# First batch's loads in groups of eight tiles, dummy matmuls among the column sums, and a third weight product on the first exponentials

## The chip, the cores and the metric

The kernel runs on one core of one Trainium2 chip. The time is the device time of one execution in microseconds (us). Before the change it is 813.8 us (median; single executions of the measurement 813.60 to 813.84). A time here is about 1.8 us longer than the span of the same execution's trace.

## The reference

Four batches. In each, a 256 x 256 channel attention: q and k are normalized over the 6016 tokens, their product goes through a softmax, and v is multiplied by it. The result goes through a gated feed-forward block.

```python
qn = q / (norm(q, axis=1) + 1e-6);  kn = k / (norm(k, axis=1) + 1e-6)   # B, N, C = 4, 6016, 256
a = softmax(kn.transpose(0, 2, 1) @ qn / tau)
x = (v @ a).reshape(B * N, C)
out = (silu(x @ w_gate) * (x @ w_val)) @ w_out                          # d_ff = 1536
```

## The kernel before

The softmax matrix is folded into the gate and value weights (`wp_matmul`), so that the tokens see only the feed-forward matmuls. Batches 1 to 3 get their softmax in the background of the batch before. The first batch can't: its k and q (12.3 MB in fp32) are loaded and cast to fp8 first, and TensorE waits for them. q and k have 47 tiles of 128 tokens; a load takes 4 tiles. All are issued from GpSimd, in this order:

```python
groups = [(s, min(4, NS - s)) for s in range(0, NS, 4)]            # NS = 47
qgroups = groups[:-1] + [(s, min(2, NS - s)) for s in range(gs, NS, 2)]
order = [k groups ...] + [q groups ...]                             # 12 + 13 loads
for ...: load_qk(0, g, which, gl)
load_first_v()
load_w(0, HW); load_w(HW, WP)         # gate and value columns 0-255, 256-511
load_v(*allc[1])                      # second chunk of v
for wc in range(1, NWC):              # first of these: "wg1", gate columns 512-1023
    load_w(wc * WP, (wc + 1) * WP)
```

As the groups land, ScalarE and VectorE square them (`first_square`), TensorE forms the logits (`gemm1_pair`, q only) and the sums of squares: with a matrix of ones for k and the first 36 tiles of q (`first_row_sums`), as columns for q's last 11 tiles (`first_col_sums`). Then comes the softmax and the first weight products:

```python
row_eps(rs); transpose_first_v(); keep_warm(3)     # keep_warm: dummy matmuls of 512 columns
... two exponentials on ScalarE ...
row_sum(0)
wp_matmul(b, 0, 0, units[0], lo); wp_matmul(b, 1, 0, units[1], lo)
row_sum(1)
... the other products, evacuations, then the feed-forward loop
```

Of the kernel before, what the change touches and what calls it, by code (L numbers as in the profile page):

```python
# [17 lines left out]
def kernel(  # L18
# [17 lines left out]
    CH = C // P  # L36
    FH = DFF // P
    NS = N // P
# [14 lines left out]
    groups = [(s, min(4, NS - s)) for s in range(0, NS, 4)]  # L53
# [45 lines left out]
    def load_qk(b, g, which, gl=groups):  # L99
        if b not in qk_tiles:  # L100
            q_sb = qkpool.tile([P, NS, C], FP8, tag="q_sb")
            k_sb = qkpool.tile([P, NS, C], FP8, tag="k_sb")
            qk_tiles[b] = (q_sb, k_sb)
        gs, gm = gl[g]
        src, dst = (q, k)[which], qk_tiles[b][which]
        nc.gpsimd.dma_start(  # L106
            out=dst[:, gs:gs + gm, :],
            in_=src[b].rearrange("(p s) c -> p s c", s=NS)[:, gs:gs + gm, :])
# [17 lines left out]
    def transpose_first_v():  # L126
        vt_ps = psum_o.tile([P, CH, CS * P], BF16, tag="o")
        for h in range(CH):
            for j in range(CS):
                nc.tensor.transpose(vt_ps[:, h, j * P:(j + 1) * P],  # L130
                                    v0_sb[:, j, h * P:(h + 1) * P], ident)
        state["vt_ps"] = vt_ps
        vT_new = vpool.tile([P, CH, CS * P], BF16, tag="vT")
        vt_ready[(0, 0)] = vT_new

    def evacuate_first_v(h):
        nc.vector.tensor_copy(vt_ready[(0, 0)][:, h, :], state["vt_ps"][:, h, :])
# [43 lines left out]
    def first_row_copy(b):  # L181
        row = work.tile([1, C], FP32, tag="row")
        nc.vector.tensor_copy(row, state[b, "ss", 0][0:1, :])
        state[b, "row"] = row
# [21 lines left out]
    def first_root(dst, src):  # L206
        nc.scalar.activation(dst, src, ACT.Ln)
        nc.scalar.activation(dst, dst, ACT.Exp, scale=0.5)
# [7 lines left out]
    def first_inv_k(b, n):  # L216
        part = state[b, "ink"][:, n * (C // 4):(n + 1) * (C // 4)]
        nc.vector.reciprocal(part, part)

    def first_softmax(b):  # L220
        kq, ink = state[b, "kq"], state[b, "ink"]
        inq = work.tile([P, CH], FP32, tag="inq")
        first_root(inq, state[b, "cols"])
        s_f = work.tile([P, CH, C], FP32, tag="s_f")
        nc.vector.tensor_mul(s_f[:, 0, :], kq[:, 0, :], ink)
        nc.vector.tensor_scalar_add(inq, in0=inq, scalar1=1e-6)
        nc.vector.reciprocal(inq, inq)
        if inv_tau != 1.0:
            nc.vector.tensor_scalar_mul(inq, in0=inq, scalar1=inv_tau)
        nc.vector.tensor_mul(s_f[:, 1, :], kq[:, 1, :], ink)  # L230
        rs = psum_m.tile([P, CH], FP32, tag="misc")
        row_eps(rs)
        transpose_first_v()
        keep_warm(3)
        for h in range(CH):
            evacuate_first_v(h)
        exT = attn.tile([P, CH, C], BF16, tag="exT")
        state[b, "exT"] = exT
        for jh in range(CH):
            nc.scalar.activation(exT[:, jh, :], s_f[:, jh, :], ACT.Exp,  # L240
                                 scale=inq[:, jh:jh + 1])


        def row_sum(jh):
            for ih in range(CH):
                nc.tensor.matmul(rs[:, ih:ih + 1], exT[:, jh, ih * P:(ih + 1) * P],
                                 ones_bf[:, 0:1], start=False,
                                 stop=(jh == CH - 1), skip_group_check=True)

        units = []  # L250
        for u in range(2 * CH):
            unit_ps = psum_gv.tile([P, HW], FP32, tag="gv"[u % 2])
            units.append(unit_ps)
        row_sum(0)
        wp_matmul(b, 0, 0, units[0], lo)
        wp_matmul(b, 1, 0, units[1], lo)
        row_sum(1)
        finish_rs(b, rs)
        wp_matmul(b, 0, 1, units[0], lo)
        wp_matmul(b, 1, 1, units[1], lo)  # L260
        for u in (2, 3):
            for jh in range(CH):
                wp_matmul(b, u, jh, units[u], lo)
        for u in range(4):
            wp_evacuate(b, u, units[u], lo, u % 2 == 1)
        for u in range(2):
            wp_unit(b, u, psum_o, "o", hi)
        nc.scalar.preload_act_table(ACT.Silu)
# [85 lines left out]
    def row_eps(rs):  # L354

        nc.tensor.matmul(rs, ones_f[0:1, :], eps[0:1, :], start=True, stop=False,
                         skip_group_check=True)
# [10 lines left out]
    def finish_rs(b, rs, eps=0.0):  # L368
        smr = work.tile([P, CH], FP32, tag="smr")
        if eps:  # L370
            nc.vector.tensor_scalar_add(smr, in0=rs, scalar1=eps)
            nc.vector.reciprocal(smr, smr)
        else:
            nc.vector.reciprocal(smr, rs)
        Wg = attn.tile([P, CH, DFF], BF16, tag="Wg")
        Wv = attn.tile([P, CH, DFF], BF16, tag="Wv")
        state[b, "smr"], state[b, "W"] = smr, (Wg, Wv)

    def keep_warm(n):
        ps = psum_o.tile([P, 2, C], FP32, tag="o")  # L380
        for _ in range(n):
            nc.tensor.matmul(ps, ones_bf, warm_bf, start=True, stop=True)
# [4 lines left out]
    full, lo, hi = slice(0, WP), slice(0, HW), slice(HW, WP)  # L387

    def wp_matmul(b, u, jh, ps, part):
        wc, w, ih = wp_units[u]  # L390
        cols = slice(wc * WP + part.start, wc * WP + part.stop)
        nc.tensor.matmul(ps, state[b, "exT"][:, jh, ih * P:(ih + 1) * P],  # L392
                         (w_gate_sb, w_val_sb)[w][:, jh, cols],
                         start=(jh == 0), stop=(jh == CH - 1))

    def wp_evacuate(b, u, ps, part, on_dve):
        wc, w, ih = wp_units[u]
        scale = state[b, "smr"][:, ih:ih + 1]
        cols = slice(wc * WP + part.start, wc * WP + part.stop)
        dst = state[b, "W"][w][:, ih, cols]  # L400
        if on_dve:
            nc.vector.tensor_scalar_mul(dst, in0=ps, scalar1=scale)
        else:
            nc.scalar.activation(dst, ps, ACT.Copy, scale=scale)

    def wp_unit(b, u, pool=psum_m, tag="misc", part=full, on_dve=None):

        ps = pool.tile([P, part.stop - part.start], FP32, tag=tag)
        for jh in range(CH):
            wp_matmul(b, u, jh, ps, part)  # L410
        wp_evacuate(b, u, ps, part, u % 2 == 1 if on_dve is None else on_dve)
# [117 lines left out]
    VT_AHEAD = 2  # L529


    NG = len(groups)
    gs, gm = groups[-1]
    qgroups = groups[:-1] + [(s, min(2, NS - s)) for s in range(gs, NS, 2)]
    NQ = len(qgroups)
    order = [(g, 1, groups) for g in range(NG)] + [(g, 0, qgroups) for g in range(NQ)]
    for n, (g, which, gl) in enumerate(order):
        load_qk(0, g, which, gl)
        if n == 8:
            make_identity(nc, identf)  # L540
            nc.gpsimd.memset(half, 0.5)
            nc.gpsimd.memset(minus, -1.0)
# [6 lines left out]
    nc.gpsimd.dma_start(out=w_out_sb, in_=moe_w_out.rearrange("(h l) d -> l h d", l=P))  # L549
    G_COLS = NQ - 4  # L550
    T_COLS = qgroups[G_COLS][0] // 2
    for g, which, gl in order:
        gs, gm = gl[g]
        ts = list(range(gs // 2, (gs + gm + 1) // 2))
        if which == 0 and g == NQ - 1:
            continue
        if which == 0 and g == NQ - 2:

            gs, gm = gl[g + 1]
            ts += range(gs // 2, (gs + gm + 1) // 2)  # L560
        if which == 0 and g == G_COLS:
            first_row_copy(0)
        sqs = [first_square(0, t, which, on_dve=(t % 2 == 1)) for t in ts]
        if which == 0:
            for t in ts:
                gemm1_pair(0, t)
            if g == G_COLS:
                first_cols(0)
        for t, sq in zip(ts, sqs):
            if which == 0 and g >= G_COLS:  # L570
                first_col_sums(0, t, sq)
            else:
                first_row_sums(0, t, which, sq, (T_COLS if which == 0 else NP) - 1)
        if which == 0:
            if g == 0:
                first_norm_k(0)
                nc.vector.tensor_copy(ident, identf)
            elif g <= 4:
                first_inv_k(0, g - 1)
    first_softmax(0)  # L580
    prev = None
    for gi, (b, ci) in enumerate(allc):
# [56 lines left out]
```

## Time and profile before

| | before |
|---|---|
| time, median | 813.8 us |
| span of the trace | 811.9 us |
| TensorE busy | 98% |
| last landing of q | 34.07 us |
| wg1 landed, TensorE continuous from there | 40.55 us |
| TensorE's wait for wg1 | 0.38 us |

The lines that this rests on are in the prediction. One more view matters afterwards: the windows view over stretches of 3.41 us, which is the step in which the granted clock changes in these traces. The columns are the stretch, its length, busy us (and instructions) of TensorE, weight loads, VectorE, ScalarE, GpSimd, then the granted clock, DMA share and GB/s written.

```profile
25.06:28.47 3.41, 3.14 (x24) 2.12 (x22) 2.71 (x5) 1.89 (x3) 1.59 (x3) 1.00 1.11 104
28.47:31.89 3.42, 2.94 (x20) 1.85 (x19) 1.65 (x4) 1.26 (x2) 1.61 (x3) 1.00 1.12 108
31.89:35.30 3.41, 3.13 (x40) 2.62 (x40) 2.38 (x5) 2.23 (x5) 2.51 (x4) 1.00 1.26 167
35.30:38.71 3.41, 3.28 (x30) 2.29 (x32) 2.88 (x9) 2.39 (x7) 3.23 (x6) 1.00 1.27 205
```

TensorE is busy for 2.94 us or more of each 3.41 us while it waits for q, and the clock is whole (1.00).

### The profile page before, as it was taken

To read this page: it belongs to the slowest core of one execution; us is meant where nothing else is said; L and a number is where in the kernel's file an instruction comes from. 1 tells how busy PE (TensorE), PEld (TensorE's weight loads), DVE (VectorE), ACT (ScalarE), POOL (GpSimd) and SP (SyncE) were. 2 spreads that over 40 slices of the span, in tenths; PEclk is the share of its full clock that TensorE was granted. 3 is DMA by queue.
4 is the path that set the end of the run, shared out by engine and by line. 5 is a ranking of instruction groups with operands and counts; after the bars stand their busy time and mean duration, and the time that the engine had idled before them with its cause. 6 is when DMAs were issued, how large, how long until landed. Compare 5 with 4: busy or idle time off the path is not lost.

```text
span 811.9 us, 13668 instructions
## 1 busy us (share of the span) xinstructions
PE 794.1 (98%) x4952; PEld 488.9 (60%) x5042; DVE 524.3 (65%) x795; ACT 434.8 (54%) x757; POOL 267.2 (33%) x330
## 2 busy tenths in 40 slices
PE   5999999999999999999999999999999999999998
PEld 3656666665565666666565666666556565665666
DVE  4777777657556777656755677765765555555554
ACT  4666655545555556545555556654554544444543
POOL 5515887423000888722100488752300000000000
PEclk9999999999999999999999999999999999999999
DMA  9993875329312678334912377641942112112101
GB/s 87 142 157 69 115 105 86 80 34 150 77 40 46 96 100 106 74 65 95 127 40 59 53 96 112 89 78 37 171 102 66 46 50 55 52 40 65 50 27 59
DMA packets 93747, 64.99 MB, mean 80 GB/s; under 512 B 52896, under 2 KB 92448, under 8 KB 92928
## 3 DMA queue, kind: packets, MB, share of 16 engines
q0 software_dynamic: 19584, 27.41, 29.0%
q1 hardware_dynamic: 73952, 36.65, 18.2%
q8 instruction: 39, 0.64, 0.4%
q14 instruction: 28, 0.23, 0.1%
q10 hardware_dynamic: 144, 0.07, 0.0%
HBM read 79.04 MB, written 36.70 MB: 143 GB/s over the span
## 4 chain that ended last, share of the span: by engine, by line
PE 93%; DMA 4%; issue 1%; DVE 1%; POOL 0%; ACT 0%; POOLq 0%
PE o_new L457 30%; PE v_ps L423 30%; PE g_ps L423 28%; DMA q_sb<-in_q_dram 2%; PE ps L392 2%; PE kq_new L151 2%; DMA k_sb<-in_k_dram 1%; DMA w_gate_sb<-in_moe_w_gate_dram 1%; DVE sv L433 0%; POOL k_sb L106 0%; ACT silu L429 0%; PE last_ps L481 0%; POOL vb L114 0%; DVE sq L274 0%; PE kq_new L156 0%
## 5 line engine op out<-in xcount | busy, mean ns | idle before, releaser
L433 DVE TENSOR_TENSOR sv<-silu,v_ps 128x512 bf16<-128x512 bf16 (+1 forms) x576 | 388.3, 674 | 263.9 <-ACT silu L429 261.1
L429 ACT ACTIVATE silu<-g_ps 128x512 bf16<-128x512 f32 (+1 forms) x576 | 338.7, 588 | 323.4 <-PE g_ps L423 257.5
L457 PE MATMUL o_new<-w_out_sb,sv 128*128 128x256 bf16 x2244 | 337.2, 273 | 1.5
L423 PE MATMUL v_ps<-vT,Wv 128*128 128x512 bf16 (+1 forms) x1100 | 324.3, 374 | 2.9
L423 PE MATMUL g_ps<-vT,Wg 128*128 128x512 bf16 (+1 forms) x1074 | 319.1, 375 | 0.3
L457 PEld LDWEIGHTS <-sv 128*128 128x128 bf16 x2244 | 219.6, 98 | 140.6
L423 PEld LDWEIGHTS <-Wv 128*128 128x128 bf16 x1152 | 112.7, 98 | 130.7
L284 POOL TENSOR_TENSOR acc_new<-acc_new,sq 128x512 f32<-128x512 f32 x135 | 157.6, 1167 | 45.1 <-DVE sq L274 36.9
L423 PEld LDWEIGHTS <-Wg 128*128 128x128 bf16 x1152 | 109.7, 98 | 24.9
L274 DVE TENSOR_TENSOR sq<-q_sb 128x512 bf16<-128x512 fp8e5 x72 | 65.9, 915 | 0.0
L279 POOL TENSOR_TENSOR acc_new<-sq 128x512 f32<-128x512 bf16 x3 | 3.5, 1154 | 150.5 <-DVE sq L274 150.5
L275 ACT ACTIVATE sq<-k_sb 128x512 bf16<-128x512 fp8e5 x72 | 44.2, 614 | 0.0
L466 ACT COPY o_sb<-o_new 128x512 f32<-128x512 f32 x48 | 28.1, 586 | 14.9 <-PE o_new L457 14.5
L151 PE MATMUL kq_new<-k_sb,q_sb 128*128 128x512 fp8e5 x184 | 32.0, 295 | 0.5 <-DMA q_sb<-in_q_dram 0.5
L106 POOL DMA_DIRECT2D q_sb<-in_q_dram x49 | 27.4, 558 | 13.5 <-DMA k_sb<-in_k_dram 5.5
L468 DVE COPY o_sb<-o_new 128x512 f32<-128x512 f32 (+1 forms) x47 | 31.3, 666 | 0.0
L106 POOL DMA_DIRECT2D k_sb<-in_k_dram x48 | 26.0, 542 | 10.4 <-DMA w_out_sb<-in_moe_w_out_dram 5.6
L178 PE MATMUL ss_new<-sq,ones_bf 128*128 128x256 bf16 x83 | 17.8, 353 | 9.1 <-ACT sq L168 8.6
L114 POOL DMA_DIRECT2D vb<-in_v_dram x47 | 24.1, 515 | 5.3 <-DMA vb<-in_v_dram 4.1
L151 PEld LDWEIGHTS <-q_sb 128*128 128x256 fp8e5 x184 | 21.2, 138 | 2.6 <-DMA q_sb<-in_q_dram 2.0
L178 PEld LDWEIGHTS <-ones_bf 128*128 128x128 bf16 x83 | 9.9, 122 | 15.9 <-issue 11.6
L312 POOL TENSOR_TENSOR inv<-inv,half 128x4 f32<-128x4 f32 x3 | 3.1, 1036 | 36.7 <-DVE inv L311 36.7
(94 smaller groups left out, 195.9 us busy)
## 6 DMA issues: line engine op xcount, KB each, us to landing
out_dram<-o_sb SPq DMA_DIRECT2D x92, 256.0 KB, 2.5
vb<-in_v_dram POOLq DMA_DIRECT2D x43, 256.0 KB, 5.9
k_sb<-in_k_dram POOLq DMA_DIRECT2D x44, 128.0 KB, 5.9
q_sb<-in_q_dram POOLq DMA_DIRECT2D x44, 128.0 KB, 5.1
w_out_sb<-in_moe_w_out_dram POOLq DMA_DIRECT2D x1, 768.0 KB, 13.7
vb<-in_v_dram POOLq DMA_DIRECT2D x4, 192.0 KB, 3.5
vT<-vb SPq DMA_TRANSPOSE x47, 4.3
w_gate_sb<-in_moe_w_gate_dram POOLq DMA_DIRECT2D x2, 256.0 KB, 7.0
```

The source lines that it names most:

```text
L106: nc.gpsimd.dma_start(out=dst[:, gs:gs + gm, :], in_=src[b].rearrange("(p s) c -> p s c", s=NS)[:, gs:gs + gm, :])
L151: nc.tensor.matmul(kq[:, jh, :], q_sb[:, ps:ps + 2, js], k_sb[:, ps:ps + 2, :], start=(t == 0 and jh == 0), stop=last, perf_mode=DR, skip_ ...
L178: nc.tensor.matmul(state[b, "ss", which], ones_bf, sq[:, s, :], start=(t == 0 and s == 0), stop=(t == t_last and s == pm - 1))
L274: nc.vector.tensor_mul(sq[:, :pm, 0, :], q_sb[:, ps:ps + pm, :], q_sb[:, ps:ps + pm, :])
L275: nc.scalar.activation(sq[:, :pm, 1, :], k_sb[:, ps:ps + pm, :], ACT.Square)
L284: nc.gpsimd.tensor_tensor(out=acc, in0=acc, in1=sq[:, s, :, :], op=ALU.add)
L423: nc.tensor.matmul(dst[:, :mv], W[:, kk, fs], vT[:, kk, :mv], start=(kk == 0), stop=(kk == CH - 1))
L429: nc.scalar.activation(silu[:, :mv], g_ps[:, :mv], ACT.Silu)
L433: nc.vector.tensor_mul(sv[:, f, :mv], silu[:, :mv], v_ps[:, :mv])
L457: nc.tensor.matmul(self.o_ps[:, j % 2, :], self.sv[:, f, j * P:(j + 1) * P], w_out_sb[:, f, :], start=(f == 0), stop=(f == FH - 1))
L466: nc.scalar.copy(o_sb[:, :m, :], self.o_ps[:, :m, :])
L468: nc.vector.tensor_copy(o_sb[:, :m, :], self.o_ps[:, :m, :])
```

## The change

The intent: fewer loads on the queue that bounds the start, TensorE kept at full clock in the thinner column-sum stage, and one more product in the wait for the second exponential.

```diff
-    qgroups = groups[:-1] + [(s, min(2, NS - s)) for s in range(gs, NS, 2)]
+    kgroups = [(s, min(8, NS - s)) for s in range(0, NS, 8)]
+    ...  size = 8 if rest >= 16 else 4 if rest >= 4 else min(2, rest)   # q: 8 8 8 8 4 4 4 2 1
@@ first_softmax
+        keep_warm(1)
         row_eps(rs)
         transpose_first_v()
-        keep_warm(3)
+        keep_warm(2)
@@
         wp_matmul(b, 1, 0, units[1], lo)
+        wp_matmul(b, 2, 0, units[2], lo)
         row_sum(1)
         ... (the remaining products follow, as before)
@@ loop over the groups
+            if G_COLS <= g < NQ - 2:
+                keep_warm(1)
```

More of the change, by code (lines that the diff above doesn't have):

```diff
@@ L256, in first_softmax @@
         wp_matmul(b, 1, 0, units[1], lo)
+        wp_matmul(b, 2, 0, units[2], lo)
         row_sum(1)
         finish_rs(b, rs)
-        wp_matmul(b, 0, 1, units[0], lo)
-        wp_matmul(b, 1, 1, units[1], lo)
-        for u in (2, 3):
-            for jh in range(CH):
-                wp_matmul(b, u, jh, units[u], lo)
+        for u, jh in ((0, 1), (1, 1), (2, 1), (3, 0), (3, 1)):
+            wp_matmul(b, u, jh, units[u], lo)
         for u in range(4):
@@ L529 @@
     VT_AHEAD = 2
-    NG = len(groups)
-    gs, gm = groups[-1]
-    qgroups = groups[:-1] + [(s, min(2, NS - s)) for s in range(gs, NS, 2)]
-    NQ = len(qgroups)
-    order = [(g, 1, groups) for g in range(NG)] + [(g, 0, qgroups) for g in range(NQ)]
+    kgroups = [(s, min(8, NS - s)) for s in range(0, NS, 8)]
+    qgroups, at = [], 0
+    while at < NS:
+        rest = NS - at
+        size = 8 if rest >= 16 else 4 if rest >= 4 else min(2, rest)
+        qgroups.append((at, size))
+        at += size
+    NG, NQ = len(kgroups), len(qgroups)
+    order = [(g, 1, kgroups) for g in range(NG)] + [(g, 0, qgroups) for g in range(NQ)]
     for n, (g, which, gl) in enumerate(order):
         load_qk(0, g, which, gl)
-        if n == 8:
+        if n == 4:
             make_identity(nc, identf)
```

## The prediction

> **What bounds the kernel now.** I read the page first. Its head, busy time and chain say that TensorE is the bound of the whole program, but that four hundredths of the span belong to transfers:
>
> ```profile
> span 811.9 us, 13668 instructions
> PE 794.1 (98%) x4952; PEld 488.9 (60%) x5042; DVE 524.3 (65%) x795; ACT 434.8 (54%) x757; POOL 267.2 (33%) x330
> PE 93%; DMA 4%; issue 1%; DVE 1%; POOL 0%; ACT 0%; POOLq 0%
> ```
>
> 811.9 us of span stand for 813.82 us of time; the 1.9 us between them I take as constant. The change touches only the first batch, so next I read the chain in order of time over the first 75 us:
>
> ```profile
> 1.22 3.34 POOL k_sb L106 x6
> 4.56 8.36 DMA k_sb<-in_k_dram
> 12.92 0.28 issue
> 13.21 9.44 DMA q_sb<-in_q_dram
> 22.64 0.28 issue
> 22.93 10.19 DMA q_sb<-in_q_dram
> 33.12 0.28 issue
> 33.40 0.53 POOL vb L114
> 33.93 0.10 issue
> 34.03 6.52 DMA w_gate_sb<-in_moe_w_gate_dram
> 40.55 0.04 issue
> 40.60 1.04 PE ps L392 x4
> 41.63 0.43 PE g_ps L423 x2
> ```
>
> The reader is to see one border, at 40.55 us. Before it nothing but loads sets the pace: k, q, then the load of the gate weights' columns 512 to 1023, which is called wg1 here. After it TensorE runs without a gap, and nothing of the change reaches there. So the change is worth exactly what it moves wg1's landing, as long as TensorE has come to its wait before that. The timeline gives the slack (columns: start us, us, engine, line, operation, then what it waited for):
>
> ```profile
> 38.75 0.60 PE L392 MATMUL ps<-w_val_sb,exT 128*128 128x256 bf16 x4
> 39.62 0.59 PE L423 MATMUL v_ps<-vT_new,Wv 128*128 128x512 bf16 x2
> 40.60 1.04 PE L392 MATMUL ps<-w_gate_sb,exT 128*128 128x512 bf16 x4 [0.38 <-DMA w_gate_sb<-in_moe_w_gate_dram]
> ```
>
> TensorE stood idle for 0.38 us before wg1: that is all that work on TensorE could grow by without cost, and work taken away there gives nothing. Last, two stretches of the windows view (busy us of each engine, granted clock, DMA share, GB/s written) and the GpSimd issues in the timeline:
>
> ```profile
> 15.00:20.00 5.00, 4.31 (x18) 2.44 (x18) 2.55 (x5) 2.52 (x4) 2.16 (x5) 1.00 1.13 104
> 25.00:30.00 5.00, 4.64 (x35) 3.17 (x33) 3.46 (x6) 2.52 (x4) 2.50 (x4) 1.00 1.13 108
> ...
> 20.47 0.53 POOL L106 DMA_DIRECT2D q_sb<-in_q_dram  x1 [0.71 <-DMA q_sb<-in_q_dram]
> 21.68 0.53 POOL L106 DMA_DIRECT2D q_sb<-in_q_dram  x1 [0.68 <-DMA q_sb<-in_q_dram]
> ...
> 30.50 0.70 POOL L524 DMA_DIRECT2D w_gate_sb<-in_moe_w_gate_dram  x1 [0.53 <-DMA q_sb<-in_q_dram]
> ```
>
> The transfer engines are never empty (share over 1, packets overlap), and their 104 GB/s of fp8 written are 416 GB/s of fp32 read. Each GpSimd issue waits for the landing of the load eight issues before it: from 20.47 to 30.50 us eight landings of 4 tiles come at a pitch of (30.50 - 20.47) / 8 = 1.254 us. So loads in flight are plenty, and the bound of this stage is the rate of the queue.
>
> **What the Trainium skill says.** "DMA: Bandwidth & Descriptors", section Specifications, has a fabric ceiling of 435 GB/s over 16 engines. The trace agrees: a 4 KB read takes 173 ns, a 1 KB read 60 ns in the packet records, which is 37.7 ns per KB and engine, 16 x 1024 B / 37.7 ns = 435 GB/s, plus 22 ns. The same page, Rules for kernel authors, asks for at least 1 MiB per DMA; a 4-tile load reads 512 KB, an 8-tile load 1 MiB. But its fit of about 2.0 us fixed plus bytes over 436 GB/s is for one DMA alone (section Anatomy of one DMA); with eight in flight this trace shows only 1.254 us per 512 KB, so nearly all of that fixed part is hidden already, and the rule's gain with it. "TensorE: Matmul & The Clock Gate", Part 1, says that the array runs at half clock until it has been busy for a window of about 3.4 us, and falls back after an idle one. The trace agrees on the first: the four row-sum matmuls of a load span 1.01 us until 20 us and 0.60 us from 24 us on; the clock's record starts at 21.65 us. It never falls before the end.
>
> **The change, part by part.**
>
> Loads of eight. k goes from 12 loads to 6, q from 13 (eleven of 4 tiles, then 2 and 1) to 9 (8, 8, 8, 8, 4, 4, 4, 2, 1): ten loads fewer, the same bytes. What a load costs beside its bytes comes from the landing records, as the first engine sees them: pitch 1.254 us for 4 tiles, 0.96 for 3, 0.66 for 2, 0.34 for 1. The slope is (1.254 - 0.34) / 3 = 0.305 us per tile (eight packets of 1 KB of source per engine at 37.7 ns make 0.301), so the rest is 1.254 - 4 x 0.305 = 0.035 to 1.254 - 4 x 0.301 = 0.05 us per load. I choose 0.04, and check it on the value chunk's load, 512 KB in one 32 KB read per engine, which lands 1.24 after its predecessor: even very long packets gain only 0.015. Ten loads fewer: 10 x 0.04 = **0.4 us**, all of it on the path: last q landing from 34.07 to 33.7 us, wg1 from 40.55 to 40.15. The weight loads that follow are unchanged in count, order and size. Issues wait for the load eight before, as now, so the queue holds more bytes, not fewer; GpSimd's 0.53 us per issue stays hidden, and is paid ten times less.
>
> Granularity. The last fifteen q tiles keep their 4, 4, 4, 2, 1, so what follows the last landing is as before. In the stages ahead an 8-tile group comes each 2 x 1.254 - 0.04 = 2.47 us. ScalarE and VectorE have two squares each in it, 2 x 0.63 and 2 x 0.69 us. TensorE has 8 logits matmuls and 8 row sums, twice what a 4-tile group has, at full clock 2 x (0.5 + 0.43) = 1.9 us; at half clock about 4 us. The first q group lands 1 us later (21.2 instead of 20.2 us), finds TensorE cold, and a backlog of one or two us builds until the clock rises, somewhere from 24.6 to 28 us. At a gain of 0.6 us per group it is worked off by the column sums unless the window falls badly. The four buffers of squares now are one group, not two; squares start again as row sums free them.
>
> Dummy matmuls. One each after the column sums of two groups, 0.22 us at full clock, in gaps where TensorE waits for q (the chain shows loads there); the second may push the last logits matmuls by up to 0.2 us. One moves ahead of the transposes, where TensorE now waits 0.26 us for v: hidden, and it leaves two instead of three after them, 0.2 us off the way to the first row sum. Together about zero.
>
> Third product. The two exponentials take 0.91 us from 35.77 us, so TensorE waits for the second until 36.68 us; with one dummy fewer there is room of 0.4 us, which the two old products fill by 0.2. The third (0.11 us) fits, and is 0.11 us less afterwards. It stands ahead of the wait for wg1, so it adds to the 0.38 us of slack and not to the time.
>
> Sum: 813.82 - 0.4 - 0 - 0 = **813.4 us**.
>
> **The rivals.**
>
> (a) Long packets run much better, as the rule of 1 MiB suggests, and the stage gains 1 us or more. Against it: at 0.301 us per tile the 25 loads can't take less than 47 x 2 x 0.301 = 28.3 us, and from the first landing on they take 28.6 us at the slowest engine for the 90 tiles after the first load, 0.6 of which an instruction fetch of 16 KB took at 30 us from one engine. There is no microsecond to win but that one. If the fetch falls on an engine that is ahead (the engines' landings of one load lie 0.75 us apart), some 0.5 us more come: 812.9.
>
> (b) TensorE becomes the bound: cold for longer in q, or throttled again between bursts of 2.5 us, so that it reaches wg1's wait late. If it warms at 28 us, it is 0.9 us late at the last q group; less 0.38 of slack that costs 0.5: 813.9. A fall of the clock at the softmax would cost more, some 1 to 1.5 us: 814.5. For it: 68% busy in the k stage didn't raise the clock. Against it: the clock never fell in the column-sum stage of before, and the dummies were put there for it.
>
> (c) The loads gain, but a new wait for another load sets the start, and nothing moves: 813.8. The weight loads stand in the same queue behind q and move with it, so I hold this for unlikely.
>
> **Range and chances.** The middle is 813.4; rival (a) with the fetch bounds it at 812.8 below, (b) in its mild form at 814.0 above; the runs of before lie within 0.24 us. 2% would be 16 us, and the whole stage before 40.55 us holds no such amount to win and no mechanism to lose it. Faster 0.01, same 0.98, slower 0.01.
>
> **What would show it.** Right: the chain still changes from loads to TensorE at a wait for wg1, near 40.15 us; GpSimd issues in the k stage at a pitch of 2.46 to 2.48 us; TensorE waits there 0.2 to 0.6 us; the third product lies ahead of the second row sum, without delaying it by more than 0.1 us. Wrong: a pitch under 2.4 us (packets gain more than their fixed part), the chain running through logits matmuls or column sums in 22 to 35 us (rival b), a granted clock under 1 after 28 us, or wg1's landing unmoved though the pitch fell (rival c).

## The result

| | before | changed |
|---|---|---|
| executions, us | 813.60 813.72 813.77 813.81 813.82 813.84 | 813.38 813.44 813.67 813.73 815.01 815.38 |
| median, us | 813.79 | 813.70 |
| ratio | | 1.0004 (95% interval 0.9991 to 1.0017) |
| span of the trace, us | 811.9 | 811.6 |

A ratio is the mean time of one kernel's runs over that of the other's in the same rounds, so it isn't quite the ratio of the medians. Here the means are 814.10 and 813.76 us: the two executions at 815 pull the ratio over 1, though four of six are faster than the median of before, and two of these faster than all of it. Executions over 1.5% slower than the fastest of the same kernel are left out of the means.

The profile of the changed kernel (813.38 us). First the page's first line and the shares of the chain:

```profile
span 811.6 us, 13660 instructions
PE 93%; DMA 4%; issue 1%; DVE 0%; POOL 0%; ACT 0%; POOLq 0%
```

Then pieces of the chain in order of time (start us, us, what):

```profile
3.50 12.81 DMA k_sb<-in_k_dram
16.59 16.18 DMA q_sb<-in_q_dram
...
33.70 6.58 DMA w_gate_sb<-in_moe_w_gate_dram
40.29 0.05 issue
40.33 1.04 PE ps L391 x4
```

The form is that of before: loads up to wg1, then TensorE. The border went from 40.55 to 40.29 us, by 0.26, and the span from 811.9 to 811.6. Next, in the timeline, two issues of GpSimd, the third product with the row sum behind it, and TensorE's wait for wg1:

```profile
14.14 0.53 POOL L106 DMA_DIRECT2D q_sb<-in_q_dram  x1 [1.95 <-DMA k_sb<-in_k_dram]
16.59 0.53 POOL L106 DMA_DIRECT2D q_sb<-in_q_dram  x1 [1.92 <-DMA k_sb<-in_k_dram]
...
36.45 0.27 PE L391 MATMUL unit_ps<-w_val_sb,exT 128*128 128x256 bf16 x1
36.57 0.20 PE L247 MATMUL rs<-ones_bf,exT 128*128 128x1 bf16 x2
...
40.33 1.04 PE L391 MATMUL ps<-w_gate_sb,exT 128*128 128x512 bf16 x4 [0.40 <-DMA w_gate_sb<-in_moe_w_gate_dram]
```

The pitch of 8-tile landings is 16.59 - 14.14 = 2.45 us (2.46 as the mean of the four from 6.75 us on), where two 4-tile loads took 2.51. The third product stands ahead of the second row sum (36.45 against 36.57 us). The wait for wg1 is 0.40 us, as before. So the mechanism is there. What doesn't fit is the size (0.26 us in this trace, where 0.40 was predicted) and the pair of executions at 815 us.

**Where the other 0.14 us are.** A load is complete when the last of 16 transfer engines has landed its share, and the trace records each engine's landing. This table is worked out from those records: the first engine's landing in us, then how far behind it the other engines came, the last four of them.

```
load                           first   13th  14th  15th  16th
before,  q tiles 32-35         29.46   0.42  0.60  0.63  0.75
before,  q tiles 36-39         30.71   0.57  0.60  0.70  1.32
before,  wg1                   39.44   0.63  0.76  0.81  1.11
changed, q tiles 36-39         30.18   0.52  0.54  0.57  0.63
changed, q tiles 40-43         31.42   0.53  0.56  0.63  1.34
changed, wg1                   38.96   0.48  0.57  0.72  1.33
```

Within one load a single engine falls back by 0.6 us or more, and stays back (the DMA share is over 1 from 5 us on, so the queue is never empty). In the same moment (29.97 us before, 30.45 us changed) the trace has a 16 KB packet on the instruction queue, taking 0.94 us. At the 37.7 ns per KB of the prediction 16 KB are 0.60 us of one engine. The first engine gained 39.44 - 38.96 = 0.48 us, and 0.22 of it was lost because the last engine is now 1.33 us behind instead of 1.11.

### The profile page after: what moved, and what is told of

Same layout as the page of the kernel before. It is cut to its first block, busy times and chain, and to the rows that moved or that the text cites. A ratio compares the mean times of both kernels' runs of the same rounds, so it can differ in the third digit from the quotient of the medians.

```text
span 811.6 us, 13660 instructions
## 1 busy us (share of the span) xinstructions
PE 791.4 (98%) x4953; PEld 488.7 (60%) x5044; DVE 523.9 (65%) x795; ACT 433.6 (53%) x757; POOL 262.4 (32%) x320
## 4 chain that ended last, share of the span: by engine, by line
PE 93%; DMA 4%; issue 1%; DVE 0%; POOL 0%; ACT 0%; POOLq 0%
PE o_new L456 30%; PE v_ps L422 30%; PE g_ps L422 29%; PE ps L391 2%; DMA q_sb<-in_q_dram 2%; PE kq_new L151 2%; DMA k_sb<-in_k_dram 2%; DMA w_gate_sb<-in_moe_w_gate_dram 1%; DVE sv L432 0%; ACT silu L428 0%; POOL k_sb L106 0%; PE last_ps L480 0%; PE kq_new L156 0%; POOL vb L114 0%; DVE sq L273 0%
## 5 line engine op out<-in xcount | busy, mean ns | idle before, releaser
L106 POOL DMA_DIRECT2D q_sb<-in_q_dram x45 | 25.2, 561 | 14.7 <-DMA k_sb<-in_k_dram 9.8
L106 POOL DMA_DIRECT2D k_sb<-in_k_dram x42 | 22.8, 544 | 12.0 <-DMA w_out_sb<-in_moe_w_out_dram 5.6
L178 PE MATMUL ss_new<-sq,ones_bf 128*128 128x256 bf16 x83 | 14.8, 335 | 10.9 <-ACT sq L168 10.9
```

The source lines that it names most:

```text
L106: nc.gpsimd.dma_start(out=dst[:, gs:gs + gm, :], in_=src[b].rearrange("(p s) c -> p s c", s=NS)[:, gs:gs + gm, :])
L178: nc.tensor.matmul(state[b, "ss", which], ones_bf, sq[:, s, :], start=(t == 0 and s == 0), stop=(t == t_last and s == pm - 1))
```

## The experiments

All runs gave a correct result. In each traced execution where TensorE waited for wg1, the span less wg1's last landing is 771.3 us, so the start alone decides the time. Executions near 814.5 us and above are called long.

### The two halves of the loads, and the whole again

`e1_again` is the changed kernel unaltered.

> The changed kernel unaltered, for the share of its longer executions. It had two kinds: four of six at 813.4 to 813.7 us and two at 815.0 and 815.4 us, these with mean clocks of 0.993 and 0.996, about three and two cold windows of 3.41 us. Theory A (k in eights: bursts raise the clock early and let it fall just as q begins), theory B (q in eights: the first q group comes 1 us later to a cold TensorE and its backlog reaches the wait for wg1) and theory C (the clock falls in column sums or softmax) all expect two kinds again, a fifth to a half of the executions near 815. If all are at 813.4 to 813.7, the longer ones were the chip and not the kernel.

Measured: 813.16 813.18 813.63 813.67 814.00 us, median 813.63, before beside it 813.78; ratio 0.9996. No long one in five, but one in nine of before (814.93): long executions are not the change's own.

`e2_k4q8` loads k in fours:

```diff
-    kgroups = [(s, min(8, NS - s)) for s in range(0, NS, 8)]
+    kgroups = [(s, min(4, NS - s)) for s in range(0, NS, 4)]
```

> The changed kernel with k in fours, q in eights: four merges of ten are left, so at 0.05 us each some 0.3 us of the gain is given back: 813.6 to 813.9 where undisturbed. Theory A: no executions near 815, as the k stage is that of before and its clock never rose early. Theory B: as many near 815 as in the changed kernel. Theory C: as many.

Measured: 813.54 to 813.94 us, median 813.84, ratio 0.9998; no long one.

`e3_k8q4` loads q in fours:

```diff
-        size = 8 if rest >= 16 else 4 if rest >= 4 else min(2, rest)
+        size = 4 if rest >= 4 else min(2, rest)
```

> The changed kernel with q in fours, k in eights: six merges are left, 813.4 to 813.8 us where undisturbed. Theory A: executions near 815 remain. Theory B: they vanish, as a 4-tile q group comes 1.2 us earlier and finds less waiting. Theory C: they remain.

Measured: 813.59 to 813.77 us, median 813.67, ratio 0.9997; no long one.

As `e1_again` has no long execution either, these runs can't tell theories A and B apart. Both need long executions that follow the grouping, and nothing here supports that. wg1's first landing was 39.18 us with six loads fewer (`e3_k8q4`), 0.26 earlier than before, which is 0.043 per load; with four fewer (`e2_k4q8`) it was 39.45, no gain: there the k stage itself ended 0.13 us later than before at the first engine, and one engine was already 1.2 us behind the first at 8 us. I have no cause for that.

### Without the dummy matmuls

`e4_nodummy` is the changed kernel with `keep_warm(3)` after the transposes as before, and no dummies among the column sums:

```diff
-            if G_COLS <= g < NQ - 2:
-                keep_warm(1)
-        keep_warm(1)          # ahead of row_eps
-        keep_warm(2)
+        keep_warm(3)
```

> The changed kernel without its dummy matmuls among the column sums, three after the transposes as in the kernel before. Theories A and B: the same share near 815 and the same 813.4 to 813.7 otherwise, at most 0.1 us apart, since the dummies lie in gaps. Theory C: more executions near 815 or above, mean clock under 0.998 in them, and a trace with a cold window between 30 and 40 us.

Measured: 812.87 to 813.35 us, median 813.09, ratio 0.9990. No expectation held: it was the fastest yet, 0.5 us below `e1_again` on the same chip. In its trace the 16 KB packet fell on the engine that was first (after it, the landings of the others lie 0.15 us nearer to the first), so wg1's last landing was only 0.73 us behind (39.79 us), and TensorE came to wg1 with no wait of its matmuls. The trace explains its own execution, but not why five in a row were fast.

### Third product and dummies alone, on the kernel before

`e5_third` adds the third product to the kernel before, `e6_dummy` all of the dummies; each is that part of the diff above.

> The kernel before with the third product alone. Theory 1 (the time is wg1's landing at its last engine plus 771.3 us, and work of TensorE ahead of it lies in slack): no change, 813.6 to 813.9 us, the wait for wg1 about 0.1 us longer than 0.38. Rival (TensorE's chain is what counts, and the product shortens it): 813.7 or less by 0.1.

Measured: 813.40 813.69 813.89 814.06 814.74 us, ratio 1.0001.

> The kernel before with the dummy matmuls alone. Theory 1: no change, 813.6 to 813.9 us, the wait for wg1 shorter by up to 0.2 us. Rival (the dummies among the column sums hold up the last logits matmuls and with them the start): 814.1 to 814.4 us, as the changed kernel was 0.5 us above the one without them.

Measured: 813.67 to 814.24 us, median 813.75, ratio 0.9999.

Neither moves the time, as Theory 1 has it. wg1's last landing was 40.82 and 40.59 us, with spans of 812.1 and 811.9. The dummies cost nothing in the kernel before, so the rival of 814.1 us falls. They do use up slack: TensorE's wait for wg1 is 0.12 us with them, where it was 0.38.

### Is it the instruction fetch?

`e7_startdummy` is `e4_nodummy` with two dummies ahead of the first k square (`keep_warm(2)`), which gives back the TensorE instructions that were taken out.

> The changed kernel without dummies among the column sums, but with two dummies ahead of the first k square, where TensorE idles: as many TensorE instructions as the changed kernel. Theory 2 (what the dummies changed is which transfer engine the 16 KB instruction fetch near 30 us falls on relative to the others, not TensorE's work): any value from 812.9 to 813.7 us, decided by whether the fetch's engine was behind; wg1's last landing less its first 1.1 us or more if slow and 0.8 or less if fast. Rival (the dummies themselves cost): 813.1 us as without them, whatever the spread.

Measured: 813.17 813.23 813.26 813.43 814.50 us. wg1 came 1.06 us after its first engine, and the span was 811.4. Between the two forecasts, so it decides nothing.

`e9_start30` moves the fetch on purpose. In the traces it comes when some 218 to 237 records of TensorE instructions have gone by (171 in the one slow execution, `e11_loads` below), and then once in 208 to 300. Thirty matmuls of one column in TensorE's idle time at the start bring it forward by 60 instructions:

```diff
+    for _ in range(30):
+        nc.tensor.matmul(small_ps[:, 0, 0:1], ones_bf, warm_bf[:, 0:1], start=True, stop=True)
```

> The changed kernel without dummies among the column sums, with 30 one-column matmuls ahead of the first k square, where TensorE idles: 60 TensorE instructions earlier. Theory 2 (a 16 KB instruction fetch comes with the same TensorE instruction each time, after some 225 of them, and puts one of the 16 transfer engines back by 0.6 to 0.75 us for good): the fetch moves from 30 us to 25 to 27 us, and the load in whose landings one engine suddenly lags moves with it. The lag then stays until wg1, so the time remains in 812.9 to 813.7 us. Rival (the lag comes at a fixed time, or with the first weight loads): it stays at 30 us.

Measured: 813.14 813.31 813.41 813.42 814.00 us. The 16 KB packet came at 25.24 us instead of about 30, and the lag moved with it:

```
e9_start30                     first   13th  14th  15th  16th
q tiles 16-23                  25.33   0.35  0.47  0.50  1.94
q tiles 24-31                  27.79   0.34  0.44  0.46  1.14
wg1                            39.03   0.43  0.46  0.79  1.19
```

The rival (a fixed time, or the weight loads) falls. The fetch is what puts one engine back, and it goes with TensorE's instruction count. In the load during which it happens the engine can be 1.9 us late, and it keeps 0.6 to 0.7 us of that.

### wg1 ahead of the second value chunk

`e8_vlater` takes away the wait for wg1 by another order of the queue, on top of `e4_nodummy`:

```diff
-    load_v(*allc[1])
     for wc in range(1, NWC):
         load_w(wc * WP, (wc + 1) * WP)
+        if wc == 1:
+            load_v(*allc[1])
```

> The changed kernel without dummies among the column sums, and the second value chunk's load behind wg1 and its twin instead of ahead. wg1 then lands 1.25 us earlier. Theory 1: TensorE no longer waits for wg1 at all; the start is TensorE's own chain from the last q landing, so 812.7 to 813.1 us, and scatter from the fetch is smaller. If the time stays at that of the changed kernel without dummies in every execution, TensorE's chain was the bound there already; if it rises over 814, the value chunk's transposes come too late near 52 us.

Measured: 817.76 to 822.19 us, median 820.54, ratio 1.0075 (every execution is longer than all of before). A clear miss, and the last of the listed outcomes. In the chain in order of time:

```profile
34.71 7.00 DMA vb<-in_v_dram
41.71 0.02 issue
41.73 16.62 DMA vT<-vb
```

And in the waits of TensorE (who waited for whom: us in total, times, longest us):

```profile
PE g_ps L421 <- DMA vT<-vb: 5.6, 1, 5.6
```

The chunk landed at 41.7 us instead of 39.3. Its transposing transfer then took 16.6 us among the other transfers, and TensorE waited 5.6 us for it at the second chunk. In the kernel before that transfer was done at 48.4 us, for a use at 52.7: the order of the queue had little room there, which I hadn't looked at closely enough. At wg1 itself the theory held: it landed at 39.04 us, and TensorE came without a wait, at 40.46.

### Larger groups still, the loads alone, and the repeat

`e10_k16` is `e4_nodummy` with k in sixteens (`min(16, NS - s)`, squares still in chunks of four pairs). `e11_loads` is `e4_nodummy` without the third product. `e12_nodummy2` is `e4_nodummy` unaltered.

> The changed kernel without dummies among the column sums, k loaded in sixteens (3 loads instead of 6), squares still in fours of pairs. Theory 1 with 0.047 us per load that is saved: first engine's landing of wg1 0.14 us earlier than with k in eights (38.98 to 38.84 us), time 812.9 to 813.1 us. Rival (TensorE, which starts later on k and is cold, now sets the pace): 813.5 us or more, with logits matmuls or row sums in the chain of 20 to 35 us.

Measured: 813.15 813.38 813.84 814.39 814.57 us, ratio 0.9998. wg1's first landing was 38.90 us, 0.13 earlier than with k in eights, as forecast. The time was not: no execution is in 812.9 to 813.1, and the median 813.84 with logits matmuls in the chain from 32.21 us is what the rival listed. The traced execution was a long one, though, and the chain enters TensorE after a late q load, not in the k stage as the rival had it.

> The loads in groups alone: neither dummies moved nor the third product. Theory 1: as with the third product, 813.0 to 813.4 us, since the product is in slack. Rival (the third product is what lets TensorE reach wg1 in time once wg1 comes early): 0.1 us above the run beside it that has it.

Measured: 813.15 813.23 813.23 813.43 us, and one of 2990.16 us, which was the traced one; nothing is compared with it. The other four, at the times of the same kernel with the third product (below), fit the loads alone giving all of the gain; none of them is traced.

> The changed kernel without dummies among the column sums, again and on the same chip as the three beside it, to see whether it repeats as the fastest so far. If its 813.09 us was more than luck of which engine the fetch fell on: 812.9 to 813.3 us. If it was that luck: 813.2 to 813.7 us, like the changed kernel.

Measured: 813.08 813.27 813.32 813.59 us and one of 816.04, the traced one. The median is at the border of the two forecasts and decides nothing. The profile of a long execution was had twice. The windows view of `e12_nodummy2`, TensorE alone (stretch, length, busy us and instructions, granted clock, DMA share, GB/s):

```profile
30.56:33.98 3.42, 2.40 (x27) 1.00 1.17 143
33.98:37.39 3.41, 3.19 (x32) 0.50 1.43 220
37.39:40.80 3.41, 3.41 (x18) 0.50 1.12 185
```

In its timeline, the wait in the first of these stretches:

```profile
32.27 0.65 PE L151 MATMUL kq_new<-k_sb,q_sb 128*128 128x512 fp8e5 x4 [1.02 <-DMA q_sb<-in_q_dram]
```

And of `e10_k16`, all engines:

```profile
30.89:34.30 3.41, 2.30 (x31) 1.83 (x30) 2.31 (x5) 1.78 (x3) 1.85 (x3) 1.00 1.22 156
34.30:37.71 3.41, 3.19 (x25) 2.53 (x24) 1.84 (x6) 1.28 (x4) 3.36 (x6) 0.50 1.31 206
```

The clock fell to half for two stretches (6.8 us) and for one, and TensorE's chain through column sums, transposes and softmax took the place of the wait for wg1. Each fall follows a stretch in which TensorE was busy for only 2.40 or 2.30 us of 3.41. What made it idle in `e12_nodummy2` stands in the timeline: 1.02 us of waiting for q tiles 36 to 39, ahead of 32.27 us. That load landed 1.97 us after its first engine; it was the load that the instruction fetch had hit. `e10_k16` has the same picture (1.97 us, a wait of 1.11). So in both executions a fetch, a wait and a fall of the clock follow on each other.

That is a sequence, not yet a rule. `e8_vlater`, `e14_colsonly` and `e15_splitonly` (the last two below) had the same load 1.80 to 1.98 us late and waits of 1.12, 1.05 and 1.04 us, and their clock stayed whole until 57 us or to the end. Nor does the busy time decide: `e8_vlater` has a stretch of 2.30 us and `e15_splitonly` one of 2.38 with no fall after them.

The traces hold ten more falls, one in each of ten traces (the changed kernel's own is at 19.35 us), all in the k stage or at its end, after stretches with 1.4 to 1.7 us busy. A count orders all of them better: the output columns of the matmuls that start in a stretch (256 for a logits or a row-sum matmul, 512 for a dummy, one for a column sum). Of the 100 stretches at whole clock that begin by 38 us in the 17 traces, twelve are followed by a fall, and these have 2048 to 3084 columns; four with 2844 to 3102 columns held, and so did all 84 with 3328 or more. A column-sum stage is busy with few columns: `e10_k16` had 2324 in the stretch before its late fall, `e12_nodummy2` 3084, the kernel before 3102. With the column-sum dummies the least in the stretches that begin from 22 to 38 us is 3614 to 5140 in seven traces, without them 2324 to 4620 in ten. No run tests this count, some matmul records can be missing from a trace, and the changed kernel's two long executions had these dummies; what decides is left open.

### What the dummies cost

Four kernels on one chip: the changed kernel (`e13_again3`), only its dummies among the column sums (`e14_colsonly`), only the one moved ahead of the transposes (`e15_splitonly`), neither (`e16_nodummy3`).

> The changed kernel unaltered, beside the three below. If its dummies cost: median 813.5 to 813.8 us, 0.3 to 0.5 above the run without any. If chance between calls: within 0.15 us of that run.

> The changed kernel with the two column-sum dummies, but three dummies after the transposes as in the kernel before. If the column-sum dummies cost by holding up the last logits matmuls: as the changed kernel, 813.5 to 813.8 us. If the moved one does: 813.1 to 813.3.

> The changed kernel without column-sum dummies, but with one of the three moved ahead of the transposes. If the column-sum dummies cost: 813.1 to 813.3 us. If the moved one does: 813.5 to 813.8.

> The changed kernel without column-sum dummies and with three after the transposes, as measured twice: 813.0 to 813.4 us where the clock stays whole. An execution over 814.4 us is to show a mean clock of 0.994 to 0.996 if it is the profiled one, and in its trace a half-clock window between 30 and 41 us after a window in which TensorE was busy under 2.5 of 3.41 us.

```
                executions, us                          median
before          813.60 to 813.94 (nine)                 813.81
e13_again3      813.21 813.33 813.49 813.62 813.65      813.49   ratio 0.9997
e14_colsonly    813.16 813.24 813.33 813.61 813.64      813.33   ratio 0.9995
e15_splitonly   813.32 813.34 813.35 813.59 814.68      813.35   ratio 0.9998
e16_nodummy3    812.98 813.07 813.28 813.33 813.48      813.28   ratio 0.9993
```

Side by side on this chip all the dummies together cost 0.2 us, and neither kind stands out; `e1_again` and `e4_nodummy`, side by side on another chip, were 0.54 apart. So with the merged loads the medians differ by 0.2 to 0.5 us, and five executions a kernel don't settle how much of it the dummies cost. How they can cost is seen in the trace of `e14_colsonly`, where TensorE and not wg1 was last. Two pieces of its chain are the column-sum dummies:

```profile
33.59 0.24 PE ps L380
34.46 0.24 PE ps L380
```

There wg1 landed at 40.37 us and TensorE came to it at 40.50, without a wait. In the three traces of the changed kernel TensorE did wait for wg1, 0.4 us each, so there the dummies cost nothing.

They gave nothing in time that shows: long executions are two of sixteen of the changed kernel in all its measurements, one of fifteen of the same kernel without dummies, three of 44 of the kernel before.

The version with no dummies but the three after the transposes is the best that was run: median of its fifteen executions (`e4_nodummy`, `e12_nodummy2`, `e16_nodummy3`) 813.27 us, the changed kernel's sixteen 813.63. Fourteen of the fifteen are under 813.60, seven of the sixteen, and two of the 44 of the kernel before. Each ratio's interval contains 1 (that of `e16_nodummy3` is 0.9981 to 1.0006). It is not free of long executions.

## Why the prediction was right or wrong

**The bound** was right: the time is wg1's last landing plus 771.3 us, in every trace in which TensorE waited for it.

**Loads of eight, 0.4 us**, was right in mechanism, and in size at the first engine. With ten loads fewer wg1's first landing is at 39.03 us (mean of the nine traces with these groups and whole clock, from 38.91 to 39.09), against 39.45 in the three with the old groups: 0.43 us. Of the changed kernel's sixteen executions in all measurements, thirteen gained 0.1 to 0.6 us on the 813.8 of before; the median gained 0.17.

**The step that failed** is that this gain is "all of it on the path": the working takes the last engine's distance from the first as fixed, wg1 simply "from 40.55 to 40.15". It was 1.11 us in the trace of before, but 0.73 to 1.50 in the others, as the fetch of TensorE's instructions falls on an engine that was ahead or behind. Rival (a) had seen the fetch, and counted it only as a chance to gain 0.5 us. In the changed kernel's own trace it took 0.22 of 0.48. A lag that varies by 0.8 us from kernel to kernel is twice the effect that was forecast. The three traced executions of the changed kernel are among its faster ones (813.18 to 813.38 us); what took the gain of those at 813.6 to 813.7 us, this lag or TensorE's chain with the dummies, is not traced.

**Rival (a)** was rightly thought little of, but by a sum that doesn't fit: it sets the 28.3 us of all 94 tiles against the 28.6 us measured for 90. For 90 tiles it is 90 x 0.301 = 27.1, so 1.5 us were to be had and not 0.3: 0.6 of the fetch and some 0.9 of what the loads cost beside their bytes.

**Rival (b)** was set too low. Its "68% busy in the k stage didn't raise the clock" holds for the one trace of before (the windows view gives 10.40 of 14.00 us there, 74%); in `e5_third`, with the same k loads, the clock is whole from 13.29 us on. Its form "throttled again", with "814.5", was dismissed because the clock had never fallen in the one trace of before. It falls now and then with these kernels, as the two traced long executions show. Two of the first six executions of the changed kernel were long, and they made the ratio 1.0004, where the other four alone have 0.9997 and 0.9995 was forecast. Those two were not traced. Their mean clocks (0.993 and 0.996) are like those of the traced long ones (0.994 and 0.996), but `e1_again` had 0.996 at 813.18 us too, with its half-clock stretches in the k stage, where they cost nothing. So that these two were falls of the clock at the softmax is likely and not shown. Nor is it shown that the change makes such falls more or less frequent.

**The dummies, about zero**: 0.2 to 0.5 us between medians, against the kernel; "hidden" fails where TensorE comes last to wg1, as in `e14_colsonly`. **The third product, nothing on the path**: right (`e5_third`, `e11_loads`). **Granularity**: the first q group landed at 20.92 us (forecast 21.2) and did find a half clock, from 19.35 to 22.77 us, after a whole one. This is the rise and fall of theory A, but at 25.88 us TensorE waited for q again, so no backlog reached wg1.

**Left open**: what exactly makes the clock fall; why the first measurement had two long executions of six and the later ones none of ten; why `e2_k4q8` had an engine late from 8 us on and gained nothing from four loads fewer; and the execution of 2990 us.

## What to carry to other kernels

When a stage is bound by a full queue, count what one load costs beside its bytes from the pitch of landings under load, here 0.04 us: merging loads wins only that. A wait for a load is a wait for its slowest engine; look at the first and the last landing before trusting a gain under a microsecond. And ask how many executions a tail needs: six with two outliers had turned a gain of 0.2 us into a loss.

## What the Trainium skill lacked or had wrong

- "Runtime: NRT & Kernel Launch", section Instruction fetch mechanics, says that instructions are refilled in blocks of 16 KiB and that the cost is mostly hidden. The block size agrees: 16 KB packets, the first after 218 to 237 records of TensorE instructions. What it lacks is the cost to loads in flight, and no other page has it: the packet takes 0.94 us of a transfer engine that carries the kernel's loads, that engine is 0.6 us or more behind from then on, and the load of that moment lands up to 1.98 us behind its first engine (`e15_splitonly`).
- "TensorE: Matmul & The Clock Gate", section Why this matters for your kernels, ties the fall to half clock to one window of idle time, and asks for no gaps over about 3 us. Here it fell after stretches of 3.41 us with 2.40 and 2.30 us busy, in which the longest waits of the matmuls were 1.02 and 1.11 us. It held after one of 2.30 (`e8_vlater`), so a share of busy time alone is no rule either; the count of columns above orders the stretches better.
- The same page, Part 1, mentions a clock stuck at a quarter for 50 us and more. In `e11_loads` one whole execution (span 2988.4 us) looks so: row-sum matmuls start 0.42 us apart, where other traces have 0.11 at whole and 0.21 at half clock. That it was the clock is not shown, as the trace has no record of it at all.
- "DMA: Bandwidth & Descriptors" gives a fixed cost of about 2 us for one load (section Anatomy of one DMA), and asks for 1 MiB (section Rules for kernel authors). No figure is given for loads in a full queue; here it is 0.043 us per load (ten loads fewer, 0.43 us).
